# A hand-ordered attention and feed-forward kernel: a new order list, with two groups of seven block products fewer and another opening

## The chip, the cores and the metric

The kernel runs on one core of one Trainium2 chip. The metric is the device time of one execution in microseconds (us); lower is better. The core has a TensorE for matmuls (PE; its weight loads are shown apart as PEld and overlap with the matmuls), a VectorE (DVE), a ScalarE (ACT), a GpSimd (POOL) and a SyncE (SP) that issues DMAs. Each engine works through its own instructions strictly in order. 16 DMA engines move data; DMAs are issued in the queues of SP, POOL and ACT.

## The reference

Queries and keys are each assigned to the nearest of 16 centroids of their head. Attention is taken only between queries and keys of the same cluster. The result, with the heads side by side, goes through a feed-forward layer with a SiLU.

```python
batch, n_heads, seq, head_dim = (4, 8, 768, 64); n_clusters = 16
q_assign = np.argmax(np.einsum('bhsd,hcd->bhsc', q_n, c_n), axis=-1)   # q_n, c_n: unit length
k_assign = np.argmax(np.einsum('bhsd,hcd->bhsc', k_n, c_n), axis=-1)
mask = q_assign[:, :, :, None] == k_assign[:, :, None, :]
scores = np.where(mask, scale * np.matmul(q, k.transpose(0, 1, 3, 2)), -1000000000.0)
attn = np.exp(scores - np.max(scores, axis=-1, keepdims=True))
attn = attn / (np.sum(attn, axis=-1, keepdims=True) + 1e-09)
attn_out = np.matmul(attn, v)
x = attn_out.transpose(0, 2, 1, 3).reshape(3072, 512)
h = x @ w_in            # 512 x 2048
g = h * (1.0 / (1.0 + np.exp(-h)))
out = g @ w_out         # 2048 x 512
```

## The kernel before, in words

**Order by hand.** The tile scheduler is off (`manual_schedule`). A long list of words, `order` (lines 813 to 954), is read from front to back by the loop at the end of the function; each word is looked up in the table `words` and issues the instructions of one small step. An engine gets its instructions in the order of the words that have work for it, and semaphores see to it that data are there and buffers free. So the list fixes the order on every engine and in every DMA queue, and nothing else decides when a step runs: a word runs as soon as everything ahead of it on its own engine is done and its inputs and its buffer are there, wherever it stands among words of other engines. A letter at the end of some words names the engine: A for ACT, D for DVE, P for POOL, S for SP's queue. A number behind `@` is the PSUM bank (0 to 3) that a step of PE writes.

**Attention words.** There are 32 heads (4 batches of 8), numbered i; jobs 0 to 7 and `x0`, `x1` are the first batch in smaller pieces.
- `ld.i` (`load`, line 102) asks SP for the raw q and k of a job; jobs 0 to 7 are asked for ahead of the list, job 0 in ACT's queue. Raw buffers are shared: job 8 takes the one of job 2, job 9 that of job 3, job 10 of 4, job 11 of 5, job 12 of 6; `x0` and `x1` take those of jobs 0 and 1.
- `hi.i` (line 114) copies raw to 16 bits (ACT line 120, POOL line 122 or DVE line 124); `lo.i` (DVE, line 129) makes the rest that the 16 bits leave out. Four `hl` buffers go round.
- `tr.i` (PE, line 152) transposes both and `ev.i` (ACT line 161 or DVE line 163) brings the result from PSUM to SBUF; from job 8 on `tp.i` (line 138) does both by a DMA transpose in SP's queue.
- `L.i` (PE, line 176) multiplies with the centroids; `ls`, `mx`, `ge` (DVE) add the halves, find the largest and write the one-hot code of the cluster.
- The code goes beside q and k as extra rows, so that the scores of other clusters come out far below the rest: `cd` (PE), `ce` (ACT or DVE) and `cg` (DMA, SP, line 260), or for heads 0 and 3 `ct` (PE) with `cq` (ACT) and `ck` (DVE, line 278), without a DMA; later jobs use `sc` (POOL), `cx` (SP) and `mv` (DMA from SP or POOL).
- `s.u` (PE, line 353) makes the scores of unit u (two matmuls of 384 columns), `x.u` (ACT, line 358) their exp. 192 units; in the first batch units 0 to 2 are head 0, 3 to 5 head 1 and so on up to 23, and 24 to 47 are the second half of its queries.
- `v.i` loads v (SP or POOL queue; five buffers go round) and `vc.i` (POOL, line 294) casts it; `pv` (PE, line 370) sums exp times v, `nm` (DVE) divides, `xp`/`xe` or `xd` transpose the result into the feed-forward's input.

**Feed-forward words.** The first product has 16 blocks of 128 columns for each half batch (`b.c`).
- A plain unit computes one block for 384 rows: `au.b.c.f`, or `ab` and `ae` for its first three matmuls and its last (PE, line 418), then `t` (tanh on ACT, line 438) and `g` (gate on DVE, line 441).
- A group `b.c.s` computes four blocks (columns 2s, 2s+1 and both eight further) from seven products of 2 by 2 blocks instead of eight (class `Quad`): `q...1` to `q...7` (PE, line 547, four matmuls of 192 columns each), `qc` (copies, ACT line 557 or DVE 559), `qa` (sums, DVE line 564), `qt` and `qg` (tanh on ACT, line 571, gate on DVE, line 584), or `qz` (ACT, line 576) at the end. It needs sums of weight blocks (`un`, DVE) and differences of input blocks (`tt`, DVE, line 507).
- `b` and `be` (plain), or the `Pair` steps `ps`, `pp`, `p1`, `pa`, `pu`, `pc`, `pd` make the second product; `bs`, `pf`, `pe`, `pm`, `py` store.
- `w.0` to `w.7` load the eight pieces of w_in, `w.8` to `w.11` the four of w_out, by POOL's queue; `w.10.22` first waits for the exp of unit 22 on POOL, and `w.11.23` for that of unit 23.

`j.3` are three idle matmuls, `cn`, `c5`, `kd`, `sk` prepare the centroids, `od` clears a code buffer on POOL.

## Time and profile before

| what | value |
|---|---|
| median of 3 runs | 295.29 us (294.81 to 296.18) |
| the profiled execution | 294.78 us |
| its span | 292.9 us |
| instructions | 8949 |
| PE busy | 283.7 us, 97% |
| DVE busy | 260.1 us, 89% |
| ACT busy | 246.8 us, 84% |
| POOL busy | 62.9 us, 21% |
| moved by DMA | 45.21 MB, mean 154 GB/s |

The profile is of one execution. Its time is 1.9 us more than its span; that part lies around the span and is in no view. PE's busy time counts matmuls whose ends are modelled, so that a stretch shown as busy can hide short gaps. In the views below an engine name with a q (SPq, POOLq) is its queue of issues and waits; `out<-in` are the program's names of tiles; a number in brackets after `<-` is idle time of the engine just before an instruction, with what ended it.

### The profile page before, as it was taken

The numbers are of one execution on the slowest core, as the hardware profiler recorded it, in microseconds if no ns is written. First come the engines' busy times: TensorE is split into PE (matmuls) and PEld (weight loads), VectorE is DVE, ScalarE is ACT, GpSimd is POOL, SyncE is SP. The second block draws the span as 40 slices with busy tenths as digits, with TensorE's granted clock in tenths as the row PEclk, the third lists the DMA queues.
The fourth block names the chain that finished last, engine by engine and source line by source line (L and its number), as shares of the span: only waits on it lengthen the run. The fifth ranks groups of instructions, "written<-read, shape, count | busy, mean of one in ns | idle before, by whom it ended". The sixth has DMA issues, their size and how long they took to land.

```text
span 292.9 us, 8949 instructions
## 1 busy us (share of the span) xinstructions
PE 283.7 (97%) x3561; PEld 222.8 (76%) x3561; DVE 260.1 (89%) x579; ACT 246.8 (84%) x430; POOL 62.9 (21%) x118
## 2 busy tenths in 40 slices
...
GB/s 212 301 212 145 174 217 287 192 187 231 234 264 140 202 223 236 188 185 82 198 147 221 185 230 218 133 77 52 187 63 66 2 113 24 87 2 36 39 40 142
DMA packets 80394, 45.21 MB, mean 154 GB/s; under 512 B 58368, under 2 KB 76736, under 8 KB 80352
## 3 DMA queue, kind: packets, MB, share of 16 engines
...
## 4 chain that ended last, share of the span: by engine, by line
PE 72%; DMA 9%; DVE 7%; ACT 7%; SPq 2%; issue 2%; ACTq 0%; DVEq 0%
PE po L683 18%; PE pS L353 16%; PE pO L370 10%; PE qa L547 8%; DMA raw<-in_k_dram 8%; PE ph L418 6%; PE qg L547 4%; PE po L596 4%; ACT P L358 3%; PE psN L176 2%; PE qb L547 2%; DVE hl L129 2%; SPq L108 1%; DMA raw<-in_q_dram 1%; ACT hl L120 1%
## 5 line engine op out<-in xcount | busy, mean ns | idle before, releaser
L358 ACT ACTIVATE P<-pS 128x768 f16<-128x768 f32 x192 | 150.4, 821 | 14.5 <-PE pS L353 12.7
L353 PE MATMUL pS<-ab 128*128 128x384 f16 x384 | 88.4, 326 | 1.1 <-ACT P L358 0.9
L353 PEld LDWEIGHTS <-ab 128*128 128x128 f16 x384 | 34.1, 98 | 12.8 <-issue 1.9
L370 PEld LDWEIGHTS <-P 128*128 128x128 f16 x1152 | 40.1, 97 | 4.9 <-ACT P L358 0.2
L370 PE MATMUL pO<-vt,P 128*128 128x65 f16 x1152 | 41.6, 193 | 0.2
L294 POOL CAST vt<-vn 128x384 f16<-128x384 f32 x32 | 21.4, 681 | 73.8 <-PE pO L370 39.5
L683 PEld LDWEIGHTS <-gt 128*128 128x128 f16 x328 | 31.7, 98 | 4.9
L547 PEld LDWEIGHTS <-ws 128*128 128x128 f16 x352 | 30.3, 98 | 5.0 <-issue 0.8
L418 PE MATMUL ph<-xt,win_s 128*128 128x384 f16 x160 | 31.9, 326 | 0.4 <-DVE cc L564 0.4
L129 DVE SCALAR_TENSOR_TENSOR hl<-raw,hl 128x768 f16<-128x768 f32 (+3 forms) x35 | 31.4, 902 | 0.9 <-ACT hl L120 0.8
L584 DVE SCALAR_TENSOR_TENSOR gt<-tn,cc 128x384 f16<-128x384 f32 x48 | 26.4, 558 | 2.1 <-ACT tn L571 2.0
L683 PE MATMUL po<-wout_s,gt 128*128 128x256 f16 x216 | 27.5, 273 | 0.0
L571 ACT ACTIVATE tn<-cc 128x384 f32<-128x384 f32 x48 | 25.3, 534 | 2.3 <-DVE gt L584 1.1
L547 PEld LDWEIGHTS <-win_s 128*128 128x128 f16 x264 | 22.9, 98 | 4.1 <-issue 0.3
L596 PE MATMUL po<-wout_s,gt 128*128 128x512 f16 x96 | 24.5, 379 | 0.1
L418 PEld LDWEIGHTS <-win_s 128*128 128x128 f16 x160 | 15.4, 98 | 9.9 <-issue 0.6
L441 DVE SCALAR_TENSOR_TENSOR gt<-tn,ph 128x384 f16<-128x384 f32 x40 | 21.7, 548 | 0.7 <-ACT tn L438 0.3
L547 PE MATMUL qa<-tt,ws 128*128 128x192 f16 x176 | 21.4, 246 | 0.4 <-ACT cc L557 0.4
L438 ACT ACTIVATE tn<-ph 128x384 f32<-128x384 f32 x40 | 20.1, 509 | 0.9 <-PE ph L418 0.6
L176 PEld LDWEIGHTS <-ab 128*128 128x128 f16 x458 | 16.8, 97 | 4.0 <-DMA ab<-hl 0.4
L220 POOL TENSOR_SCALAR od<-od 128x96 f16<-128x96 f16 x16 | 8.7, 547 | 47.2 <-DVE od L213 47.1
L382 DVE TENSOR_TENSOR xn<-pO,zr 128x384 f16<-128x384 f32 x32 | 17.8, 558 | 1.1
...
## 6 DMA issues: line engine op xcount, KB each, us to landing
raw<-in_k_dram SPq DMA_DIRECT2D x31, 192.0 KB, 4.0
out_dram<-ot SPq DMA_DIRECT2D x23, 256.0 KB, 2.4
raw<-in_q_dram SPq DMA_DIRECT2D x24, 192.0 KB, 4.3
vn<-in_v_dram SPq DMA_DIRECT2D x21, 192.0 KB, 4.2
vn<-in_v_dram POOLq DMA_DIRECT2D x11, 192.0 KB, 4.5
win_s<-in_moe_w_in_dram POOLq DMA_DIRECT2D x8, 256.0 KB, 6.8
...
cp<-gt SPq DMA_DIRECT2D x4, 256.0 KB, 4.7
```

The source lines that it names most:

```text
L129: nc.vector.scalar_tensor_tensor(out=hl[:, s, 1, :], in0=raws[job.name][:, s, :], scalar=QS, in1=hl[:, s, 0, :], op0=ALU.mult, op1=ALU.sub ...
L176: nc.tensor.matmul(L[:, n % g, :, n // g], ab[:, i, :], stk[:, job.groups[i // 3][0], x : x + w], start=(x == 0), stop=(x + w == 2 * HC),)
L353: nc.tensor.matmul(pS[:, e, 0:HALF], abs_[kj.name][:, kn, :], rhs, start=True, stop=True)
L358: nc.scalar.activation(out=P, in_=pst.pop(u)[:, :, 0:HALF], func=AF.Exp, bias=0.0, scale=ESC)
L370: nc.tensor.matmul(o[:, (2 * t + h) * VW : (2 * t + h + 1) * VW], Ps[i + h, c, j // 2][:, j % 2, ts(t, 128)], vtb[(i + h) % 13][:, j, 0:VW ...
L418: nc.tensor.matmul(ph[:, 0:HALF], win_s[:, r, ts(fb, 128)], xts[b, c][:, r, :], start=(r == 0), stop=(r == NR - 1))
L441: nc.vector.scalar_tensor_tensor(out=gt[:, fb, :], in0=tn, scalar=1.0, in1=ph[:, 0:HALF], op0=ALU.add, op1=ALU.mult)
L547: nc.tensor.matmul(o[:, g * QT : (g + 1) * QT], w, y, start=(k in (1, 2, 5) and g == 0 and r == 0), stop=(r == 1), skip_group_check=True,)
L571: nc.scalar.activation(out=t, in_=self.src(n), func=AF.Tanh, bias=0.0, scale=1.0)
L584: eng.scalar_tensor_tensor(out=self.gt[:, f : f + 2, h], in0=self.tn[n].rearrange("p (g n) -> p g n", g=2), scalar=1.0, in1=self.src(n).re ...
L596: nc.tensor.matmul(po, gts[b, c][:, fc, ts(t, 128)], wout_s[:, fc, :], start=(fc == 0), stop=(fc == NFB - 1))
L683: nc.tensor.matmul(o, l[:, f, :], x, start=(f == 0 and k in begins), stop=(f == HK - 1), skip_group_check=True)
```

## The change

Only the list `order` changes (lines 813 to 954, 1796 words, become 813 to 952, 1774 words). No function is touched.

- The groups 0.0.0 and 0.0.1 go (22 groups become 20): 14 `q` words, six `qc`, six `qa`, eight `qt`, eight `qg`, and the four `tt.0.0`. In their place stand eight plain units, `au.0.0.0` to `3` and `8` to `11`, with their `t` and `g`. The `un` words stay, since later groups use the same sums.
- The opening is in another order. `s.0` stands ahead of `L.2` and `tr.5`. `hi.5` and `hi.6` go from ACT to POOL. `v.1` and `v.10` come first among the loads of v, `v.10` from POOL. `w.1` is POOL's second DMA, `w.4` and `w.6` follow behind `hi.6` and `v.3`, then `w.0`, `w.5`, `w.3`, `w.2`, `w.7`; `w.9` and `w.8` stand behind `vc.7`, `w.10` and `w.11` later still. `ld.8`, `ld.9`, `ld.11` move up between `cg.1` and `v.2` in SP's queue.
- Steps change engine. `hi`: 18 on ACT, 14 on DVE, 3 on POOL become 12, 18, 5. `ce`: 10 on ACT and 6 on DVE become 8 and 8. `qc`: 37 and 29 become 33 and 27. `xe`: 5 and 5 become 4 and 6. One `be` goes to DVE. `v`: 21 by SP and 11 by POOL become 14 and 18. `mv`: 7 by SP and 9 by POOL become 2 and 14.
- The rest of the list holds the same steps in another order, with other banks. At the end the pair `3.1.x` is stored (`pe.3.1.x`) just ahead of the last product of the pair `3.1.p`; before, that store stood earlier.

The beginning and the end of the list:

```diff
@@ -811,146 +811,144 @@
 
     order = """
-        hi.0.A.K lo.0.K hi.0.A.Q lo.0.Q tr.0.q@1 hi.1.A j.3@2 cn tr.0.k@3 hi.2.A ev.0.k.A c5@02 lo.1 kd sk ev.0.q.A
-        v.4.S lo.2 hi.4.A hi.3.P v.0.S tr.1.kq@32 ld.x0 L.0.16@0 ev.1.k.D ev.1.q.A v.1.S tr.2.kq@13 mx.0 v.5.S ge.0
-        L.1.16@2 ev.2.k.A lo.4 v.2.S ct.0@01 ev.2.q.A mx.1 cq.0 ge.1 L.2.16@3 ck.0 hi.5.A cd.1 tr.4.kq@01 vc.4 ce.1.A
-        lo.5 ev.4.q.A cg.1 vc.0 lo.3 hi.7.A tr.5.kq@21 ld.x1 mx.2 s.0 ev.5.k.A ev.5.q.D s.1 ge.2 tr.3.kq@12 ev.4.k.D
-        vc.1 x.0 cd.2 lo.7 v.3.P L.4.16@0 ce.2.A ev.3.q.A ev.3.k.D cg.2 tr.7.kq@32 hi.6.A hi.x0.P mx.4 L.3.16@1 v.6.S
-        ge.4 ev.7.q.A lo.6 v.7.S cd.4 x.1 s.2 L.5.16@2 ce.4.D x.2 ev.7.k.D od.0 cg.4 s.3 tr.6.kq@03 mx.3 x.3 hi.x1.P
-        ld.8 ge.3 s.4 ev.6.k.D x.4 ev.6.q.D s.5 mx.5 L.6.16@1 ge.5 x.5 s.6 mx.6 cd.5 w.3 ct.3@03 x.6 ge.6 lo.x0 cd.6
-        vc.2 s.7 cq.3 s.8 w.0 x.7 ce.5.D tr.x0.k@0 ck.3 vc.5 cg.5 L.7.32@2 ce.6.A vc.3 ls.7 pv.0.0.0.x@3 x.8 cg.6 s.9
-        vc.6 mx.7 tr.x0.q@1 x.9 w.1 ge.7 s.10 ev.x0.q.D cd.7 vc.7 pv.0.0.1.x x.10 ev.x0.k.D s.11 w.2 lo.x1 pv.0.0.2.x
-        ce.7.A w.5 L.x0.32.0.6@1 x.11 L.x0.32.6.12 cg.7 s.12 w.9 ls.x0 w.7 pv.2.0.0.x@0 x.12 s.13 mx.x0 w.6 pv.2.0.1.x
-        x.13 ge.x0 w.4 pv.2.0.2.x nm.0.0 cd.x0 s.14 w.8 ce.x0.A tr.x1.k@2 x.14 s.15 cg.x0 ev.x1.k.D x.15 s.16
-        tr.x1.q@3 x.16 L.x1.32.0.6@1 s.17 ev.x1.q.D x.17 L.x1.32.6.12 s.18 ls.x1 pv.4.0.0.x@2 x.18 nm.2.0 s.19
-        pv.4.0.1.x x.19 mx.x1 s.20 xp.2.0@3 pv.4.0.2.x ge.x1 x.20 xe.2.0.D xp.0.0@0 s.21 nm.4.0 s.22 x.21 pv.6.0.y.0@3
-        xe.0.0.D x.22 xp.4.0@2 s.23 xe.4.0.D ab.0.0.7@0 hi.8.D x.23 w.10.22 cd.x1 s.24 pv.6.0.y.1 x.24 w.11.23 s.25
-        nm.6.0 ab.0.0.6@2 x.25 s.26 ce.x1.D xp.6.0@3 x.26 cg.x1 s.27 xe.6.0.D ld.11 q.0.0.0.1@1 ae.0.0.6 x.27 tt.0.0.3
-        ld.10 qc.0.0.0.1.A v.10.S s.30 ae.0.0.7 tt.0.0.1 tt.0.0.2 tt.0.0.4 q.0.0.0.2@3 t.0.0.6 qa.0.0.0.1 g.0.0.6
-        t.0.0.7 g.0.0.7 un.1.0 un.1.1 s.28 x.28 ab.0.0.5@3 ae.0.0.5 t.0.0.5 g.0.0.5 q.0.0.1.1@0 x.30 ab.0.0.4@2
-        ae.0.0.4 q.0.0.0.5@3 qt.0.0.0.0 un.2.0 q.0.0.0.6 ld.9 v.17.S un.2.1 t.0.0.4 s.29 un.4.0 qc.0.0.0.5.A un.3.0
-        s.34 q.0.0.0.3 qc.0.0.0.2.A g.0.0.4 q.0.0.0.7 qg.0.0.0.0 qa.0.0.0.3 q.0.0.1.2@2 qc.0.0.1.1.A qa.0.0.1.1 un.3.1
-        q.0.0.1.6 x.29 ld.12 s.32 qt.0.0.0.1 qt.0.0.1.0 q.0.0.1.5@3 qg.0.0.0.1 au.0.0.12@2 qc.0.0.1.5.A qc.0.0.1.2.A
-        q.0.0.1.7 qg.0.0.1.0 x.32 qa.0.0.0.2 un.4.1 t.0.0.12 q.0.0.0.4 v.13.S q.0.0.1.3 qa.0.0.1.2 s.37 qa.0.0.1.3
-        qt.0.0.0.3 qg.0.0.0.3 g.0.0.12 q.0.0.1.4 qt.0.0.1.3 au.0.0.13@3 lo.8 hi.9.D tp.8 hi.10.D hi.11.A t.0.0.13
-        pv.0.1@1 qg.0.0.1.3 b.0.0.0.0@2 lo.11 g.0.0.13 tp.11 b.0.0.0.1 x.37 x.34 nm.0.1 lo.10 qt.0.0.1.1 qt.0.0.0.2
-        qg.0.0.0.2 s.33 s.31 x.33 b.0.0.0.2 x.31 lo.9 s.41 x.41 au.0.0.14@0 s.35 qg.0.0.1.1 t.0.0.14 g.0.0.14 hi.12.D
...
-        pf.3.1.x ps.3.1.p.4 pp.3.1.x.3 pd.3.1.x pe.3.1.x pa.3.1.p pu.3.1.p pp.3.1.p.7 pc.3.1.p pp.3.1.p.3 pf.3.1.p
-        pp.3.1.p.4 pl.3.1.p pz.3.1.p py.3.1.p pm.3.1.p
+        hi.0.A.K lo.0.K hi.0.A.Q lo.0.Q tr.0.q@1 v.1.S v.10.P cn hi.1.A tr.0.k@3 v.4.S ev.0.k.A lo.1 v.0.S hi.2.A lo.2
+        j.3@2 c5@03 kd tr.1.kq@32 ev.1.k.D sk w.1 ev.0.q.A ev.1.q.A L.0.16@1 mx.0 tr.2.kq@03 hi.4.A ge.0 ev.2.k.A lo.4
+        hi.3.P hi.5.P ld.x0 L.1.16@2 mx.1 ct.0@10 ev.2.q.A ge.1 ck.0 cq.0 tr.4.kq@31 ev.4.k.D cd.1 ce.1.A ld.x1 lo.5
+        s.0 L.2.16@0 mx.2 ev.4.q.A cg.1 ge.2 x.0 L.4.16@3 hi.7.A lo.3 tr.5.kq@21 cd.2 ld.8 ce.2.A cg.2 ev.5.q.D s.1
+        ev.5.k.A s.2 hi.6.P w.4 mx.4 lo.7 ge.4 tr.3.kq@10 ev.3.k.A ev.3.q.A tr.7.kq@21 lo.6 x.1 vc.1 ev.7.q.D ev.7.k.D
+        cd.4 ce.4.A ld.9 L.3.16@0 mx.3 ge.3 L.5.16@1 mx.5 x.2 cg.4 ld.11 tr.6.kq@23 ev.6.k.D v.3.P ev.6.q.D s.3 s.5
+        v.2.S w.6 L.6.16@2 x.3 vc.0 ge.5 mx.6 cd.5 ge.6 x.5 ce.5.D s.4 cg.5 v.5.S vc.4 hi.x0.P hi.x1.P L.7.32@3 cd.6
+        ce.6.D x.4 s.6 x.6 pv.0.0.0.x@1 w.0 s.8 x.8 ct.3@20 vc.10 lo.x0 w.5 w.3 s.7 pv.0.0.1.x pv.0.0.2.x od.0 cq.3
+        x.7 s.12 vc.3 ls.7 x.12 tr.x0.k@2 ck.3 s.10 mx.7 cg.6 v.6.S x.10 lo.x1 tr.x1.q@0 s.11 x.11 ge.7 cd.7 vc.2
+        ev.x0.k.D nm.0.0 tr.x0.q@2 s.9 x.9 ev.x0.q.D tr.x1.k@1 ce.7.D cg.7 s.14 x.14 L.x0.32.0.6@2 L.x0.32.6.12 s.16
+        x.16 pv.2.0.0.x@3 hi.8.D ls.x0 s.13 x.13 pv.2.0.1.x mx.x0 ge.x0 v.11.P s.15 x.15 pv.2.0.2.x s.17 x.17 cd.x0
+        ev.x1.k.D s.18 w.2 ev.x1.q.D x.18 hi.9.D ce.x0.D vc.5 pv.4.0.0.x@0 s.19 x.19 w.7 pv.4.0.1.x s.20 x.20
+        pv.4.0.2.x lo.8 nm.2.0 v.7.S s.21 x.21 xp.2.0@1 nm.4.0 xe.2.0.D cg.x0 tp.8 xp.0.0@3 xe.0.0.D s.23 x.23 ld.10
+        L.x1.32.0.6@2 L.x1.32.6.12 ls.x1 vc.6 s.22 x.22 pv.6.0.y.0@0 s.29 x.29 xp.4.0@1 xe.4.0.A vc.7 un.3.0
+        pv.6.0.y.1 s.34 mx.x1 ge.x1 ld.12 un.1.1 nm.6.0 cd.x1 ce.x1.D s.27 x.34 cg.x1 x.27 ab.0.0.7@3 xp.6.0@0
+        xe.6.0.D s.26 x.26 un.1.0 au.0.0.0@2 t.0.0.0 lo.9 tp.9 g.0.0.0 ae.0.0.7 ab.0.0.4@1 t.0.0.7 ae.0.0.4 t.0.0.4
+        g.0.0.4 s.24 x.24 s.28 un.2.0 x.28 hi.10.D hi.11.D w.9 g.0.0.7 ab.0.0.5@2 hi.12.D au.0.0.2@0 t.0.0.2 g.0.0.2
+        s.25 ae.0.0.5 x.25 t.0.0.5 g.0.0.5 w.8 s.35 au.0.0.15@1 x.35 s.30 lo.10 pv.0.1@3 t.0.0.15 nm.0.1 x.30 s.31
+        x.31 ab.0.0.6@0 ae.0.0.6 g.0.0.15 t.0.0.6 g.0.0.6 s.36 x.36 tp.10 lo.12 au.0.0.10@2 ld.14 t.0.0.10 au.0.0.9@1
+        t.0.0.9 g.0.0.9 g.0.0.10 au.0.0.1@3 t.0.0.1 g.0.0.1 s.42 s.46 x.42 L.8.32@0 ls.8 x.46 lo.11 au.0.0.13@1 ld.13
+        t.0.0.13 v.8.P g.0.0.13 au.0.0.14@2 t.0.0.14 s.32 x.32 au.0.0.11@3 t.0.0.11 mx.8 ge.8 s.39 x.39 tp.11
+        au.0.0.12@1 t.0.0.12 s.33 g.0.0.11 g.0.0.14 w.10.22 w.11.23 x.33 vc.11 tw.0.0.6 au.0.0.3@0 s.41 t.0.0.3
+        g.0.0.3 tp.12 x.41 au.0.0.8@3 g.0.0.12 t.0.0.8 g.0.0.8 vc.8 s.38 L.9.32@2 hi.13.A pv.2.1@0 x.38 s.43 x.43
+        cd.8@1 tw.0.6.2 od.1 b.0.0.0.0@3 un.4.0 nm.2.1 v.13.S ls.9 mx.9 s.37 x.37 ce.8.D b.0.0.0.1 vc.13 hi.14.D s.40
+        ge.9 lo.13 L.11.32@0 lo.14 s.47 ld.15 xp.0.1@1 ld.17 xe.0.1.D x.47 b.0.0.1.0@2 b.0.0.1.1 b.0.0.1.2 ls.11 mx.11
...
+        pp.3.1.p.1@5 pp.3.1.x.2@0 pp.3.1.p.5@6 ps.3.1.p.3 pa.3.1.x pc.3.1.x pf.3.1.x p5.3.1.p p1.3.1.p pp.3.1.p.6
+        pp.3.1.p.3 pu.3.1.p pl.3.1.p pm.3.1.p pa.3.1.p ps.3.1.x.4 pp.3.1.p.7 pc.3.1.p pf.3.1.p pp.3.1.x.4 pp.3.1.x.3
+        pd.3.1.x pe.3.1.x pp.3.1.p.4 pz.3.1.p py.3.1.p
     """.split()
```

224 lines of the change are left out of this document (110 added, 114 removed).

## The prediction

> **What bounds the kernel now.** I read the page first, then busy time by stage, the chain of waits, the timeline of the first 60 us, the DMA view of the early stretch and the groups by line. From the page:
>
> ```profile
> span 292.9 us, 8949 instructions
> ...
> PE 283.7 (97%) x3561; PEld 222.8 (76%) x3561; DVE 260.1 (89%) x579; ACT 246.8 (84%) x430; POOL 62.9 (21%) x118
> ```
>
> TensorE (PE) is busy for 97% of the span, but that is an average over stages. The busy time by stage (stretch, its length, then busy time and count of PE, PEld, DVE, ACT and POOL, the granted clock, the share of the DMA engines, GB/s) shows where the other 3% lie:
>
> ```profile
> 0.00:14.10 14.10, 10.79 (x133) 6.91 (x134) 10.03 (x41) 10.25 (x19) 5.08 (x15) 1.00 0.83 256
> 14.10:39.00 24.90, 24.24 (x406) 18.63 (x405) 20.73 (x50) 23.86 (x37) 17.87 (x25) 1.00 0.94 182
> 39.00:58.60 19.60, 18.04 (x185) 12.08 (x183) 17.93 (x40) 17.83 (x35) 0.00 (x0) 1.00 1.12 234
> 58.60:289.50 230.90, 230.60 (x2847) 185.18 (x2843) 211.38 (x452) 194.46 (x343) 39.98 (x78) 1.00 0.65 139
> 16.00:22.00 6.00, 5.93 (x104) 4.57 (x102) 5.84 (x15) 5.89 (x10) 5.97 (x5) 1.00 0.72 205
> ```
>
> From 58.6 to 289.5 us PE idles for 0.30 us of 230.90. There a new order can win next to nothing, however much it takes off ScalarE (ACT) and VectorE (DVE), and it can lose. What can be won lies earlier: 3.31 us up to the first exp at 14.1, 0.66 from there to 39, and 1.56 from 39 to 58.6. The stretch from 14.1 to 39 is as much ACT's as PE's: 23.86 of 24.90 us.
>
> What holds PE up after 39 us is in the chain of waits (start, us, what) and, below it, in the timeline (start, us, engine and operation, in brackets the idle time before it and what ended that):
>
> ```profile
> 39.48 6.45 DMA raw<-in_k_dram
> ...
> 45.95 6.77 DMA raw<-in_k_dram
> ```
> ```profile
> 52.48 1.03 DVE L124 TENSOR_SCALAR hl<-raw 128x768 f16<-128x768 f32 x2 [1.44 <-DMA raw<-in_k_dram]
> ...
> 55.28 0.48 PE L353 MATMUL pS<-ab 128*128 128x384 f16 x2 [0.65 <-ACT P L358]
> ```
>
> The chain does not run through PE here but through loads of k that are asked for at 39.48 and 45.95 us. DVE waits 1.44 us for one of them, ACT's exp comes late behind DVE, and PE waits 0.65 us for ACT. Those loads share the DMA engines with the weights. The DMA view from 21 to 55 us (q0 is POOL's queue, q1 is SP's; packets, MB and share of the engines' time, then issues with KB each and the median us to landing):
>
> ```profile
> q0 software_dynamic: 3264, 4.20, 76.1%
> q1 hardware_dynamic: 2702, 2.62, 30.5%
> ...
> win_s<-in_moe_w_in_dram POOLq DMA_DIRECT2D x8, 256.0 KB, 6.8
> ...
> raw<-in_k_dram SPq DMA_DIRECT2D x4, 192.0 KB, 8.4
> ...
> ab<-cd SPq DMA_DIRECT2D x2, 48.0 KB, 6.2
> ```
>
> and over the whole run, where most loads have no weights beside them:
>
> ```profile
> raw<-in_k_dram SPq DMA_DIRECT2D x31, 192.0 KB, 4.0
> ...
> out_dram<-ot SPq DMA_DIRECT2D x23, 256.0 KB, 2.4
> ...
> ab<-cd SPq DMA_DIRECT2D x10, 48.0 KB, 4.1
> ...
> out_dram<-ot ACTq DMA_DIRECT2D x1, 128.0 KB, 1.7
> ```
>
> **The change part by part.** *Products.* Two groups, 28 matmuls of 192 columns each, become eight plain units of four matmuls of 384 columns. The chain shows both kinds back to back:
>
> ```profile
> 80.80 0.66 PE qa L547 x8
> ...
> 83.29 1.30 PE ph L418 x8
> ```
>
> Removed are 56 x 0.66/8 = 4.62 us, added 32 x 1.30/8 = 5.20 us: **+0.6 us** of work on PE, which bounds the kernel.
>
> *ACT, DVE and POOL.* In the groups by line (count, then busy time and the mean ns of one, then idle time before them):
>
> ```profile
> L571 ACT ACTIVATE tn<-cc 128x384 f32<-128x384 f32 x48 | 25.3, 534 | 2.3 <-DVE gt L584 1.1 <-DVE cc L564 0.9
> ...
> L438 ACT ACTIVATE tn<-ph 128x384 f32<-128x384 f32 x40 | 20.1, 509 | 0.9 <-PE ph L418 0.6
> ...
> L120 ACT ACTIVATE hl<-raw 128x768 f16<-128x768 f32 (+3 forms) x18 | 13.7, 760 | 2.1 <-DMA raw<-in_q_dram 1.3 <-DMA raw<-in_k_dram 0.7
> ...
> L557 ACT ACTIVATE cc<-qa 128x384 f32<-128x384 f32 x26 | 12.5, 492 | 1.0 <-PE qa L547 0.9
> ...
> L564 DVE TENSOR_TENSOR cc<-qb,cc 128x384 f32<-128x384 f32 x22 | 12.1, 552 | 1.2 <-PE qb L547 0.8
> ...
> L124 DVE TENSOR_SCALAR hl<-raw 128x768 f16<-128x768 f32 x14 | 7.8, 562 | 1.4 <-DMA raw<-in_k_dram 1.4
> L122 POOL TENSOR_SCALAR hl<-raw 128x768 f16<-128x768 f32 (+1 forms) x3 | 7.0, 2337 | 3.1 <-DVE hl L129 3.1
> ```
>
> ACT loses six `hi` copies net (6 x 0.760 = 4.6 us) and four group copies net (4 x 0.492 = 2.0; six go, two come over from DVE); its eight tanh of groups become eight of units, 8 x 0.025 = 0.2 less. With a few small copies more it has some 7 us less to do. DVE loses the groups' six sums and those two copies (8 x 0.552 = 4.4) and takes four `hi` (4 x 0.562 = 2.2): some 2 us less. POOL takes two `hi` at 2.3 us each, seven more loads of v and five more moves of codes. Behind 58.6 us all this is worth 0, because PE covers it; it would cost up to 1 us if POOL's queue came late with a v or a code there. In the opening it counts where ACT is what is waited for.
>
> *First scores.* The timeline of the opening:
>
> ```profile
> 3.71 0.57 POOL L781 TENSOR_TENSOR cy<-cs,hf 128x1 f32<-128x1 f32 x1 [1.80 <-DVE cs L779]
> ...
> 7.38 2.16 POOL L122 TENSOR_SCALAR hl<-raw 128x576 f16<-128x576 f32 x1 [3.10 <-DVE hl L129]
> ...
> 8.37 0.69 ACT L120 ACTIVATE hl<-raw 128x576 f16<-128x576 f32 x1
> ...
> 10.92 0.62 DVE L278 TENSOR_SCALAR ab<-pC 16x256 f16<-16x256 f16 x2
> 11.05 0.69 ACT L120 ACTIVATE hl<-raw 128x576 f16<-128x576 f32 x1
> ...
> 12.85 0.51 PEld L152 LDWEIGHTS <-hl 128*128 128x128 f16 x9 [1.03 <-DVE hl L129]
> ...
> 13.37 0.81 PE L353 MATMUL pS<-ab 128*128 128x384 f16 x4
> ...
> 14.11 0.80 ACT L358 ACTIVATE P<-pS 128x768 f16<-128x768 f32 x1
> ...
> 15.76 0.77 POOL L289 DMA_DIRECT2D vn<-in_v_dram  x1
> ...
> 18.48 1.04 PE L353 MATMUL pS<-ab 128*128 128x384 f16 x4
> ```
>
> The first score needs the code that DVE writes in `ck.0`, done at 10.92 + 0.62 = 11.54. In the old list it stands behind `tr.5`, which waits 1.03 us for `lo.5` and starts at 12.85, so it comes at 13.37. The new list puts `s.0`, `L.2` and `L.4` between `cd.1` and `tr.5`, and on ACT it takes `hi.5`, `hi.7` and `ev.5.k` from ahead of the first exp. The first score can then start near 11.7 and the first exp near 12.5, and the hole in PE is filled: **-1.0 us** (0 to -1.3). `hi.5` is made on POOL now, after `hi.3`, and is ready at 7.38 + 2 x 2.16 = 11.70; ACT had it ready at 11.05 + 0.69 = 11.74. That move costs nothing as long as its data are there.
>
> *Early transfers.* `v.10` and `w.1` come first in POOL's queue, right behind `cy`, so they go out at about 4.3 and 4.9 us. In the old list POOL's first transfer was issued at 15.76. From the DMA rows above q0 moves 4.20/(0.761 x 34 us) = 0.162 MB in a microsecond of all engines, so `w.1` (256 KB) is worth 1.6 us of them; `v.10` (192 KB) at q1's 2.62/(0.305 x 34) = 0.25 MB is worth 0.8. Up to 2.4 us of transfers are set among the loads of jobs 2 to 7. The price is 0 if ACT and DVE come later than the data anyway. It is at most about 1.8, if what is left of those loads moves at half speed while POOL's run. `hi.4` starts at 8.37 without a wait now, so there is no long wait to hide it behind but some time in hand, and I take **+0.8**, near the middle. [...]
>
> *39 to 58.6 us.* `ld.8`, `ld.9` and `ld.11` move up, to where jobs 2, 3 and 5 give their buffers back, and into a stretch in which the DMA engines have room (0.72 busy from 16 to 22 us). Six of the eight w_in pieces stand ahead of POOL's `od.0` instead of none, and `w.8` and `w.9` behind them. The groups' chains of copy, sum, tanh and gate are gone from this stage. So the waits before 52.48 and 55.28 should go. Late next is DVE, with 17.93 us of work in 19.60. I take PE's visible idle time there as won: **-1.6 us** (0 to -2.6; busy time is modelled, and gaps that it hides can go too).
>
> *The end.* A 256 KB store of the other pair is now issued at about the time of the last one, and by the rows above it takes 2.4 us where that takes 1.7: **+0.3 us** (0 to 0.7).
>
> The sum is 0.6 - 1.0 + 0.8 - 1.6 + 0.3 = -0.9 us. The profiled execution took 294.78 us (its span and 1.9 around it), 0.5 below the median of 295.29. Set against the median, the forecast is **294.4 us**.
>
> **The rivals.** *A, the early transfers hide.* ACT and DVE come late enough in the opening that no load is missed, and the stage from 39 us loses its hidden gaps too: 0.6 - 1.0 + 0 - 2.6 + 0.2 = -2.8, so 292.5. For it speaks the room on the DMA engines from 16 to 22 us. Against it speak the 2.1 us that ACT's `hi` copies already wait, for loads of q and k.
>
> *B, slower, by the shared DMA engines.* `w.1` and `v.10` push the loads of jobs 3 to 7 back by 1.8 us, and nothing of the first hole is won. With them comes `cg.1`, head 1's code, which stands behind five larger loads in SP's queue, and which takes 6.2 us beside weights against 4.1. It decides from the point where that code lands after PE reaches `s.3` (18.48 now): then PE and ACT stand still, for up to 6.2 - 4.1 = 2.1 us, of which I count 1.5. 0.6 + 0 + 1.8 + 1.5 - 1.6 + 0.3 = +2.6, so 297.9. For it also speaks that `cg.6` waits behind `v.5` in SP's queue, whose buffer is free only after `vc.10`, behind two `hi` on POOL.
>
> *C, the gain only moves.* ACT is as full as PE from 14 to 39 us, so scores made sooner wait for it there, and half of the later waits come back with other names: 0.6 + 0 + 0.8 - 0.8 + 0.3 = +0.9, so 296.2.
>
> **How the numbers follow.** The forecast has a chance of 0.36, A 0.27, B 0.22, C 0.15. A measurement of this kernel tells about 0.5% (1.5 us) from no change, so faster is under 293.8 and slower over 296.8. The forecast's own range, its terms half-way to their bounds, is 293.2 to 295.7, and a quarter of it is faster. Faster: 0.27 + 0.09 = 0.36. Slower: 0.20 of the 0.22 of B and a quarter of C, 0.24. The rest, 0.40, is the same. The range reaches past A's and B's values, to 291.6 and 298.0.
>
> **What would show it.** Right: the first score near 11.7 and the first exp before 13 us, no DVE wait for raw between 45 and 58 us, PE idle for under 0.5 us from 39 to 58.6, and 0.6 us more work of PE. Wrong: ACT idle before `hi.4` for raw, `s.3` held up by a code that has not landed, the first exp later than 13.5 us, or more than 1 us of idle PE after 60 us.

## The result, and the profile after

The kernel after takes 299.25 us (median of 6 runs, 297.38 to 301.24), the kernel before, on the same chip, 295.40 (6 runs, 294.81 to 296.18). The ratio is 1.0124, with a 95% interval from 1.0078 to 1.0169: slower by 3.9 us, and outside the forecast's range. The medians here and below are over all runs, while the ratios leave out single runs more than 1.5% above the fastest of their kernel. The profiled execution of the kernel after is its longest, 301.24 us, so about 2 us of what its trace shows are not in the median.

From its page, the span and the busy times:

```profile
span 299.4 us, 8877 instructions
...
PE 285.2 (95%) x3537; PEld 223.2 (75%) x3537; DVE 260.5 (87%) x575; ACT 238.8 (80%) x416; POOL 73.0 (24%) x132
```

ACT has 8.0 us less to do (some 7 were forecast), and PE 24 matmuls fewer (56 removed, 32 added). Neither sets the time. The busy time by stage, in the columns and stretches shown of before:

```profile
0.00:14.10 14.10, 10.11 (x102) 6.26 (x103) 8.34 (x37) 8.04 (x15) 5.62 (x16) 0.98 0.80 225
14.10:39.00 24.90, 21.65 (x352) 17.00 (x351) 21.66 (x47) 19.84 (x30) 17.99 (x22) 0.87 1.00 230
39.00:58.60 19.60, 19.60 (x209) 13.26 (x207) 18.15 (x39) 19.09 (x34) 5.57 (x11) 1.00 1.20 194
...
58.60:289.50 230.90, 227.43 (x2822) 181.18 (x2820) 208.37 (x446) 191.08 (x337) 43.84 (x84) 1.00 0.63 136
```

In the stage that the change was to win, from 39 to 58.6 us, PE was busy for 18.04 us and is now for all 19.60. The opening to 39 us, which was to win 1 us, loses 0.7 and 2.6 us of busy time, and behind 58.6 us, where nothing was to be lost, 3.47 us are idle (0.30 before).

The first loss begins with the loads of job 4. From the timeline of the opening:

```profile
10.94 0.69 ACT L120 ACTIVATE hl<-raw 128x576 f16<-128x576 f32 x1 [1.94 <-DMA raw<-in_q_dram]
...
12.37 0.50 PE L267 MATMUL pC<-ident,om 128*16 128x128 f16 x6 [2.03 <-ACT ab L161]
...
13.22 3.27 POOL L122 TENSOR_SCALAR hl<-raw 128x576 f16<-128x576 f32 x2 [4.23 <-DMA raw<-in_q_dram]
...
13.54 0.81 PE L353 MATMUL pS<-ab 128*128 128x384 f16 x2
...
14.48 0.80 ACT L358 ACTIVATE P<-pS 128x768 f16<-128x768 f32 x1
```

`hi.4` waits 1.94 us on ACT for raw q, `ev.2.k`, next on ACT, starts only at 11.53, and PE waits 2.03 us for the bank that it empties. `hi.5` on POOL waits 4.23 us for its data. The first score comes at 13.54, no sooner than before (13.37). The DMA view from 3 to 15 us shows the loads late (issues, KB each, median us to landing), after:

```profile
raw<-in_k_dram SPq DMA_DIRECT2D x5, 192.0 KB, 7.3
```

and before:

```profile
raw<-in_k_dram SPq DMA_DIRECT2D x5, 192.0 KB, 3.7
```

The second loss, from the timeline of 45 to 66 us (SPq is SP's DMA queue):

```profile
45.23 12.69 SPq L138 DMA_TRANSPOSE ab<-hl  x2
...
60.24 0.44 SPq L108 DMA_DIRECT2D raw<-in_k_dram  x1
...
61.09 0.52 PE L176 MATMUL psN<-stk,ab 128*128 128x32 f16 x12 [1.18 <-DMA ab<-hl]
...
64.54 0.84 ACT L120 ACTIVATE hl<-raw 128x768 f16<-128x768 f32 x1 [3.99 <-DMA raw<-in_k_dram]
...
66.14 0.48 PE L353 MATMUL pS<-ab 128*128 128x384 f16 x2 [2.13 <-ACT P L358]
```

The transposes of jobs 9 and 10 hold SP's queue for 12.69 us (4.65 and 7.26 of issue). The loads of job 13 stand behind them, ACT waits 3.99 us in `hi.13` with its exps behind it, and PE waits twice, for the transpose and for an exp. The four pieces of w_out go out at 39.69 to 42.79, into that stretch; in the kernel before they went out at 27.49 to 36.95, and the three transposes began at 51.07 and held the queue for 8.60 us:

```profile
51.07 8.60 SPq L138 DMA_TRANSPOSE ab<-hl  x3
```

### The profile page after: what moved, and what is told of

It reads as the page before. It is cut to its first block, busy times and chain, and to the rows that moved or that the text cites. A ratio compares the mean times of both kernels' runs of the same rounds, so it can differ in the third digit from the quotient of the medians.

```text
span 299.4 us, 8877 instructions
## 1 busy us (share of the span) xinstructions
PE 285.2 (95%) x3537; PEld 223.2 (75%) x3537; DVE 260.5 (87%) x575; ACT 238.8 (80%) x416; POOL 73.0 (24%) x132
## 4 chain that ended last, share of the span: by engine, by line
PE 80%; DMA 9%; DVE 4%; ACT 3%; issue 1%; SPq 1%; POOL 1%; ACTq 0%; POOLq 0%
PE po L683 18%; PE pS L353 18%; PE pO L370 10%; PE qa L547 9%; PE ph L418 8%; PE po L596 7%; PE qg L547 4%; DMA raw<-in_q_dram 4%; DMA ab<-cd 3%; PE psN L176 3%; PE qb L547 2%; DVE hl L129 2%; DMA raw<-in_k_dram 1%; ACT P L358 1%; DVE gt L441 1%
## 5 line engine op out<-in xcount | busy, mean ns | idle before, releaser
L353 PE MATMUL pS<-ab 128*128 128x384 f16 x384 | 89.8, 329 | 3.9 <-ACT P L358 2.1
L418 PE MATMUL ph<-xt,win_s 128*128 128x384 f16 x192 | 37.9, 326 | 0.0
L129 DVE SCALAR_TENSOR_TENSOR hl<-raw,hl 128x768 f16<-128x768 f32 (+3 forms) x35 | 33.1, 948 | 3.6 <-ACT hl L120 2.6
L547 PEld LDWEIGHTS <-ws 128*128 128x128 f16 x320 | 27.4, 98 | 3.4 <-issue 0.2
L441 DVE SCALAR_TENSOR_TENSOR gt<-tn,ph 128x384 f16<-128x384 f32 x48 | 25.7, 549 | 1.3 <-ACT tn L438 1.0
L584 DVE SCALAR_TENSOR_TENSOR gt<-tn,cc 128x384 f16<-128x384 f32 x42 | 23.8, 571 | 2.2 <-ACT tn L571 2.0
L438 ACT ACTIVATE tn<-ph 128x384 f32<-128x384 f32 x48 | 24.3, 515 | 1.1 <-PE ph L418 1.0
L571 ACT ACTIVATE tn<-cc 128x384 f32<-128x384 f32 x42 | 22.0, 533 | 0.3 <-DVE cc L564 0.2
L547 PE MATMUL qa<-tt,ws 128*128 128x192 f16 x160 | 19.2, 246 | 0.0
L176 PE MATMUL psN<-stk,ab 128*128 128x32 f16 (+1 forms) x458 | 18.1, 189 | 1.2 <-DMA ab<-hl 1.2
```

Of the source, the lines that this page charges most:

```text
L129: nc.vector.scalar_tensor_tensor(out=hl[:, s, 1, :], in0=raws[job.name][:, s, :], scalar=QS, in1=hl[:, s, 0, :], op0=ALU.mult, op1=ALU.sub ...
L176: nc.tensor.matmul(L[:, n % g, :, n // g], ab[:, i, :], stk[:, job.groups[i // 3][0], x : x + w], start=(x == 0), stop=(x + w == 2 * HC),)
L353: nc.tensor.matmul(pS[:, e, 0:HALF], abs_[kj.name][:, kn, :], rhs, start=True, stop=True)
L418: nc.tensor.matmul(ph[:, 0:HALF], win_s[:, r, ts(fb, 128)], xts[b, c][:, r, :], start=(r == 0), stop=(r == NR - 1))
L438: nc.scalar.activation(out=tn, in_=ph[:, 0:HALF], func=AF.Tanh, bias=0.0, scale=1.0)
L441: nc.vector.scalar_tensor_tensor(out=gt[:, fb, :], in0=tn, scalar=1.0, in1=ph[:, 0:HALF], op0=ALU.add, op1=ALU.mult)
```

## The experiments

The theory to begin with was the first loss above: the early transfers push the raw loads back. Its rivals were the second loss (w_out and the transposes), the copies moved to POOL, and, as the runs went on, the volume of the transfers as a whole (theory D).

All kernels change the order list alone, unless said otherwise. Medians with the ratio to the kernel before on the same chip and its interval:

| kernel | us | ratio (95%) |
|---|---|---|
| after | 299.25 | 1.0124 (1.0078 to 1.0169) |
| `w.1` later | 298.96 | 1.0106 (1.0062 to 1.0151) |
| `v.10` later | 299.30 | 1.0125 (1.0089 to 1.0161) |
| both later | 298.64 | 1.0103 (1.0061 to 1.0146) |
| w_out sooner | 307.32 | 1.0404 (1.0371 to 1.0438) |
| job 13's loads sooner | 299.70 | 1.0147 (1.0098 to 1.0196) |
| both later, codes first | 299.46 | 1.0125 (1.0067 to 1.0183) |
| w_out behind exp 36 | 307.35 | 1.0396 (1.0347 to 1.0446) |
| both later, codes first, job 13's loads sooner | 299.55 | 1.0136 (1.0078 to 1.0195) |
| after, no weights loaded | 291.83 | 0.9889 (0.9858 to 0.9921) |
| before, no weights loaded | 294.18 | 0.9973 (0.9949 to 0.9998) |
| before with units | 302.09 | 1.0243 (1.0207 to 1.0278) |
| before, loads early | 294.39 | 0.9971 (0.9948 to 0.9993) |
| after, no w_in | 300.83 | 1.0144 (1.0089 to 1.0200) |
| after, no w_out | 298.40 | 1.0119 (1.0075 to 1.0164) |
| transposes late, w_out sooner | 305.11 | 1.0323 (1.0281 to 1.0365) |
| before, loads and score early | 294.57 | 0.9995 (0.9969 to 1.0021) |
| after, less asked for early | 296.69 | 1.0062 (1.0037 to 1.0087) |
| before with extra loads | 299.48 | 1.0124 (1.0083 to 1.0165) |

**The early transfers moved back.** Theory 1 was rival B's mechanism: `v.10` and `w.1` delay the raw loads.

```diff
-hi.0.A.K ... v.1.S v.10.P cn ... sk w.1 ev.0.q.A ... hi.6.P w.4 ... v.3.P ev.6.q.D
+hi.0.A.K ... v.1.S cn ... sk ev.0.q.A ... hi.6.P w.1 w.4 ... v.3.P v.10.P ev.6.q.D
```

> The kernel after, with one piece of w_in (`w.1`, 256 KB) asked for next to `w.4` and not ahead of `hi.3` on POOL. Theory 1 (the two early transfers push the loads of jobs 4 to 7 back): those loads land about 1.6 us sooner, the q part of job 4 by 9.5 us in place of 10.86, PE's hole at 10.3 to 12.4 us shrinks to about 1 us, and the time falls by 1 to 2 us, to 297.3 to 298.3. Theory 2 (what is lost is lost near 60 us, to the late w_out) and theory 3 (the loss is the move of `hi.5` and `hi.6` to POOL): the time stays within 0.5 us of 299.25.

> The kernel after, with `v.10` asked for behind `v.3` on POOL and not ahead of `hi.3`; `v.5` then takes the buffer of head 4's v and no longer that of head 10's. Theory 1: the loads of jobs 4 to 7 land about 0.8 us sooner, and the time falls by 0.5 to 1.5 us; with v.5, cg.6, v.7 no longer held by vc.10, the codes of heads 6 and 7 and the w_out pieces come sooner too, which by theory 2 gives another 1 us or more. By theory 3 the time stays within 0.5 us of 299.25.

> Both moves at once. Theory 1: no transfer of POOL's among the loads of jobs 4 to 7, which land as in the kernel before (7.7 to 11 us); no hole of PE at 10.3 to 12.4, first score near 12, granted clock 1.0 throughout; the time falls by 2.5 to 4 us, to 295.3 to 296.8. Theory 2: the opening gives under 1 us and 3 us of PE's waits near 60 us stay. Theory 3: 299.25 within 0.5.

Neither move alone, nor both, gave what theory 1 said: the medians are 0.3, 0 and 0.6 us lower, and all three ratios lie in the interval of the change. With both moved, the opening is as it should be. From the timeline of that kernel, the first score, then a later one:

```profile
11.86 0.50 PE L353 MATMUL pS<-ab 128*128 128x384 f16 x2
...
22.79 0.50 PE L353 MATMUL pS<-ab 128*128 128x384 f16 x2 [2.19 <-DMA ab<-cd]
```

The hole of 2 us is gone from 10.3 us and has come back at 20.6. There PE waits for head 2's code, asked for at 15.54 and landed at 22.75. So the place was right and the gain was not: the DMA engines still had as much to move. The copies `hi.5` and `hi.6` are still POOL's here, so they did not make the hole of the opening.

**w_out sooner.**

```diff
-w.7 ... vc.6 ... vc.7 ... hi.11.D w.9 g.0.0.7 ... g.0.0.5 w.8 s.35
+w.7 w.9 w.8 ... vc.6 ... vc.7 ... hi.11.D g.0.0.7 ... g.0.0.5 s.35
```

> The kernel after, with `w.9` and `w.8` (pieces of w_out) asked for right behind `w.7` on POOL, ahead of the casts of the v of heads 6 and 7 that wait for their data, so that they go out near 31 us and not near 40. Theory 2: the DMA transposes tp.9 and tp.10 (issues of 4.65 and 7.26 us now) take under 3 us each, the loads of jobs 13 and 14 go out before 55 us and not at 58 to 60, PE's 3.3 us of waits between 58.6 and 66 us go, and the time falls by 2 to 3.5 us, to 295.8 to 297.3. Theory 1 alone: the opening's 4 us stay and the time falls by at most 0.5 us.

The opposite of theory 2: 8 us slower than the kernel after. The pieces went out from 32.22 and met the transpose of job 8, issued at 35.44, which landed at 52.11 (at 41.19 in the kernel after); that of job 9 took 10 us of issue. PE then waited 6.36 us at once, and behind that wait the granted clock was 0.50 from 54 to 62 us, so that a part of the 8 us is matmuls at half the clock. Going out sooner meant meeting the transposes sooner.

**Single waits taken away.** In the kernel after, `ld.13` ahead of the transposes; in the kernel with both early transfers later, the codes ahead of `ld.8`, `ld.9`, `ld.11`; and all of these together.

```diff
-cg.x1 ... lo.9 tp.9 ... tp.10 ... ld.14 ... lo.11 au.0.0.13@1 ld.13
+cg.x1 ... lo.9 ld.13 tp.9 ... tp.10 ... ld.14 ... lo.11 au.0.0.13@1
```
```diff
-cg.1 ... ld.8 ce.2.A cg.2 ... ce.4.A ld.9 ... cg.4 ld.11 ... cg.5 v.5.S ... cg.6 v.6.S
+cg.1 ... ce.2.A cg.2 ... ce.4.A ... cg.4 ld.8 ... cg.5 ld.9 v.5.S ... cg.6 ld.11 v.6.S
```

> The kernel after, with the two loads of job 13 (`ld.13`) asked for ahead of the DMA transposes of jobs 9 and 10 in SP's queue and not behind them; their buffer is free since `lo.7`. Theory S (SP's queue stands in the two transposes, 4.65 and 7.26 us of issue, and ACT stands in `hi.13` behind the loads that come after them, with its exps behind it): ACT's 3.99 us of idle time before `hi.13` go, PE's 3.3 us of waits between 58.6 and 66 us fall to about 1.2 (the wait of `L.9` for its transpose), and the time falls by 2 us, to 297.2. Theory D (the DMA engines are full up to 60 us, and what one transfer wins another loses): it falls by under 0.7 us.

> The kernel with both early transfers moved back (298.64 us), and `ld.8`, `ld.9`, `ld.11` asked for behind the codes of heads 4, 5 and 6 and not ahead of those of heads 2, 4 and 5. Theory C (a code of 48 KB takes as long as the larger loads that stand ahead of it in SP's queue): the code of head 2, 7.2 us from issue to landing there, takes about 4, PE's 2.35 us wait for it at 20.4 us goes, and the time falls by 1.5 to 3 us, to 295.6 to 297.1. Theory D: another wait takes its place, and it falls by under 0.7 us.

> `w.1` and `v.10` later, the codes ahead of `ld.8`, `ld.9`, `ld.11`, and `ld.13` ahead of the transposes. If theories C and S hold, the gains add: 298.6 - 2 - 1.5 = about 295, as fast as the kernel before. By theory D it stays above 297.5.

All three stay between 299.4 and 299.7: theories S and C fall as explanations of the time, though each wait went where it was taken away. ACT's wait in `hi.13` is gone with `ld.13` early, and PE waits 1.74 us up to 64.86 for a transpose that landed at 64.81 instead. With the codes first, head 2's code takes 6.2 us in place of 7.2, and two other codes hold PE up for 2.22 us up to 32.7 and 2.24 us up to 37.3. The second of them needs 9.68 us from issue to landing.

**w_out held back.**

```diff
-hi.11.D w.9 ... g.0.0.5 w.8 s.35 ... x.36 tp.10 ... g.0.0.14 w.10.22 w.11.23 ... vc.11 tw.0.0.6
+hi.11.D ... g.0.0.5 s.35 ... x.36 w.9.36 w.8.36 w.10.36 w.11.36 tp.10 ... g.0.0.14 ... vc.11
```

> The kernel after, with the four pieces of w_out held back until the exp of unit 36 (at 51.6 us there) and not issued at 39.7 to 42.8; the copies of w_out for the later products stand behind the next exps. Theory T (the w_out pieces of POOL's queue slow the DMA transposes of jobs 9 and 10 and so SP's queue): those two take under 3 us of issue each, the loads of jobs 13 and 14 go out before 53 us, ACT does not wait for job 13, and PE's waits between 58.6 and 66 us are those for w_out alone, which lands near 62; the time falls by 1 to 3 us. If the transposes stay above 4 us each, something else slows them.

(`tw.0.0.6`, a copy of w_out, moves behind `cd.8`.) Theory T holds for the transposes and not for the time, 307.35. Before the first piece goes out at 51.80, the transposes take 2.13, 1.45 and 1.44 us of issue; behind it the next two take 4.94 and 7.13. The pieces land at 58.7 to 70.1, where PE needs them from 60. Here too the clock is 0.50 behind the waits, from 70 to 76 us.

**No weights at all.** Each piece is set to a constant by POOL where it was asked for, in both kernels.

```diff
-            nc.gpsimd.dma_start(win_s[:, r, fs], moe_w_in[128 * r : 128 * r + 128, fs])
+            nc.gpsimd.memset(win_s[:, r, fs], 0.01)
```

> The kernel after with no transfer of w_in or w_out: each piece is set to a constant by POOL where it was asked for, so 4 MB less go through the DMA engines before 62 us; all else is as in the kernel after. Theory D (up to 60 us the transfers share the engines, and what is asked for early makes the codes, loads and transposes late that are due first): PE's holes at 10.3, 28, 36.9 and 59 to 66 us nearly all go, and the kernel after is no slower than the kernel before under the same edit: 290 to 292.5. Theory Q (the order of the instructions on SP, POOL, ACT and DVE is worse in itself): at least 2 us of holes stay, and it is 2 us or more slower than the kernel before under the same edit.

> The same edit in the kernel before, for comparison: it loses the waits of its stage from 39 to 58.6 us (1.6 us visible, up to 2.6) and perhaps 0.5 in the opening: 291.5 to 293.5. By theory D it is within 1 us of the kernel after without weights or slower than that one; by theory Q it is faster than that one by 2 us or more.

This turns the order round: 291.83 against 294.18. The two intervals do not touch. Without weights the change wins 2.4 us, with them it loses 3.9. So theory Q falls: the order on the engines is not worse in itself, nor are the products. The kernel before gains less than was expected of it (294.18, where 291.5 to 293.5 was written): from 39 to 58.6 us PE still idles for 1.67 us in it. The DMA engines' share (last column but one) fits theory D; after without weights, then before without weights:

```profile
0.00:14.10 14.10, 11.28 (x150) 7.48 (x151) 9.95 (x40) 9.48 (x18) 9.08 (x18) 1.00 0.82 252
14.10:39.00 24.90, 24.40 (x392) 18.28 (x390) 23.71 (x57) 23.78 (x36) 23.83 (x27) 1.00 0.65 181
39.00:58.60 19.60, 19.18 (x195) 12.29 (x194) 18.72 (x38) 18.49 (x33) 4.75 (x8) 1.00 0.63 136
```
```profile
0.00:14.10 14.10, 10.85 (x133) 6.82 (x134) 9.95 (x40) 10.42 (x20) 6.04 (x15) 1.00 0.80 258
14.10:39.00 24.90, 23.60 (x395) 17.73 (x394) 21.96 (x47) 22.88 (x35) 22.30 (x22) 1.00 0.26 76
39.00:58.60 19.60, 17.93 (x170) 12.26 (x171) 19.12 (x43) 18.18 (x35) 3.91 (x4) 1.00 0.57 154
```

Share times length, summed to 58.6 us: 11.6 + 16.2 + 12.3 = 40.1 us of the engines without weights after, 11.3 + 6.5 + 11.2 = 29.0 before. With weights the kernel before has 11.7 + 23.4 + 22.0 = 57.1, so the weights take about 28. Before, 29 + 28 fit into 58.6 us; after, 40 + 28 do not. (Shares reach 1.20 above, so the sum is rough.) The new list asks for some 11 us worth of loads, v and transposes sooner than it was, above all between 14 and 39 us, where the weights went.

**Which weights.** The same edit for w_in alone and for w_out alone.

> The kernel after with the eight pieces of w_in set to a constant and not loaded; w_out is loaded as in the kernel after. If w_in is what costs (opening and codes, 10 to 38 us): the holes there go and those at 59 to 66 us stay, 294 to 296. If w_out beside the transposes is what costs: at least 297.5.

> The kernel after with the four pieces of w_out set to a constant and not loaded; w_in is loaded as in the kernel after. If w_out beside the transposes is what costs: the transposes of jobs 9 and 10 take under 3 us of issue each (4.65 and 7.26 in the kernel after), the waits at 59 to 66 us go, 294.5 to 296. If w_in is what costs: at least 297.5.

The two do not part the cause. Without w_out the kernel is as slow as the change; without w_in it is no faster either, but there w_out goes out sooner, so that it does not show what w_in alone costs. Without w_out the waits behind 58.6 us go (PE is busy for 7.40 of 7.40 us up to 66) and those of the opening stay. Without w_in, the pieces of w_out go out from 31.96 and meet the transposes of jobs 8 and 9, as in "w_out sooner" (its six runs spread from 296.5 to 302.4; the profile is of a long one, 302.15). The landing times of the transposes, DMA view from 35 (for no w_in: 30) to 62 us, for the kernel after, without w_out and without w_in:

```profile
ab<-hl SPq DMA_TRANSPOSE x4, 8.4
```
```profile
ab<-hl SPq DMA_TRANSPOSE x5, 3.8
```
```profile
ab<-hl SPq DMA_TRANSPOSE x4, 7.6
```

**Kept apart.** Both early transfers later, w_out whole behind `w.7`, and job 8's transpose behind the loads of jobs 10, 12 and 13.

```diff
-w.7 ... cg.x0 tp.8 ... ld.10 ... ld.12 ... cg.x1 ... lo.9 tp.9
+w.7 w.9 w.8 w.10 w.11 ... cg.x0 ... ld.10 ... ld.12 ... cg.x1 ... lo.9 ld.13 tp.8 tp.9
```

> All transfers kept, but w_out and the transposes apart: `w.1` and `v.10` later, the four pieces of w_out together right behind `w.7` on POOL (from about 30 us), job 8's DMA transpose behind the loads of jobs 10, 12 and 13 (near 44 us and not 35). If their meeting is what costs, transposes take under 3 us of issue and the time falls from 298.6 (both early transfers moved back) to 294 to 296.5. If the volume of the transfers before 60 us costs wherever it lies, waits for codes and loads from 32 to 45 us take the place of those saved: 298 or more.

305.11: the late transpose of job 8 still took 4.92 us beside the last pieces, from 50.7 us PE stood for 5.28 us behind a gate of DVE, and the clock was 0.50 from 54 to 60 us. With everything kept, no placing of w_out that I tried was better than that of the change.

**The products alone, and two parts in the kernel before.**

```diff
-q.0.0.0.1@1 ... tt.0.0.3 ... qc.0.0.0.1.A ... q.0.0.0.2@3 ... qa.0.0.0.1 ... qg.0.0.1.2
+au.0.0.0@1 t.0.0.0 g.0.0.0 ... au.0.0.8@3 t.0.0.8 g.0.0.8 ...
```

> The kernel before with the products of the change alone: its first two groups of four (seven products each) become eight plain units, set where the products of the groups stood, and the rest of the list stays. By the prediction's sum of products it does 0.6 us more work on PE; with fewer copies and sums around them it comes to 295.0 to 296.2. If it is over 297, the loss of the change is in its products; if it is under 294.5, the units were a gain that the new order spoils.

302.09, 7 us slower. By what was written ahead of the run this would put the loss into the products. The trace speaks against it, because the place is bad: the units come one behind the other and wait for a bank. From its timeline:

```profile
49.28 0.81 PE L418 MATMUL ph<-xt,win_s 128*128 128x384 f16 x4 [2.32 <-DVE gt L441]
```

And with the weights left out the new list, with the same units spread out, is the faster one. What the units are worth in the old order stays open.

```diff
-cg.1 ... ce.2.A ... cg.2 ... cg.4 ... ld.8 ... cg.5 ... ld.11 ... ld.9
+cg.1 ... ce.2.A ... ld.8 cg.2 ... ld.9 cg.4 ... ld.11 cg.5
```
```diff
-tr.5.kq@21 ld.x1 mx.2 s.0 ev.5.k.A ... vc.1 x.0
+s.0 x.0 tr.5.kq@21 ld.x1 mx.2 ev.5.k.A ... vc.1
```

> The kernel before with the loads of jobs 8, 9 and 11 asked for where the change asks for them, ahead of the codes of heads 2, 4 and 5 in SP's queue (not after head 4's, and at 39 to 46 us), and nothing else changed. Theory C (a code waits for the larger loads ahead of it): the codes of heads 2 to 6 land 1 to 4 us later, PE waits for at least one of them between 18 and 37 us, what it wins from 39 to 58 us (up to 1.6) it loses there: 295 to 297.5. Without theory C: the waits from 39 to 58 us go and nothing takes their place, 293.5 to 294.3.

> The kernel before with the loads of jobs 8, 9 and 11 early (294.39 us), and with the first score ahead of `tr.5` on PE and its exp right behind it in the list. By the prediction's step (1 us of PE's hole at 11.8 us filled) it comes to 293.4 to 293.9. If ACT, which is as full as PE from 14 to 39 us, only waits elsewhere, it stays at 294.2 to 294.6.

The early loads cost nothing here (294.39), although some 3 us of transfers (four loads of 192 KB at 0.77 us each, an estimate from the 0.25 MB in a microsecond that the prediction reads off its DMA view) come from behind 39 us into the stretch before it. PE waits for a code once, 0.45 us. The ratio, 0.9971, is the lowest of the kernels with all their work, but the kernel that adds the first score does not repeat it (294.57, 0.9995). There the first score comes at 11.91 in place of 13.37, and adds nothing. Nor do the loads win the stage from 39 us by themselves. DVE's wait of 1.44 us for raw is gone, and PE is busy for 18.23 us where it was for 18.04:

```profile
39.00:58.60 19.60, 18.23 (x185) 12.55 (x184) 18.87 (x41) 18.58 (x34) 0.00 (x0) 1.00 1.01 203
```

PE waits there for a sum (0.39 us), a gate (0.46) and a copy (0.41).

**More and less asked for early.** The last two test the volume. In the kernel after, the v of heads 10 and 11 (two loads of 192 KB) go from before 40 us to behind 64 us, `w.1` from 5 to 13 us, and `ld.8`, `ld.9`, `ld.11` stand behind the codes of heads 4, 5 and 6. In the kernel before, 1.5 MB more are loaded.

```diff
-v.10.P ... w.1 ... hi.6.P w.4 ... vc.10 ... v.11.P ... vc.11 ... vc.13
+... hi.6.P w.1 w.4 ... vc.13 v.11.P vc.11 v.10.P vc.10
```
```diff
+        nc.sync.dma_start(spare[0][:, n, :], nat(k, 20 + n, 0, 6))
...
-cg.2 ... cg.4 ... cg.5 ... cg.6
+cg.2 dd.0 dd.1 ... cg.4 dd.2 dd.3 ... cg.5 dd.4 dd.5 ... cg.6 dd.6 dd.7
```

> The kernel after, with `w.1` next to `w.4`, the v of heads 10 and 11 asked for (and cast) only behind head 13's, near 66 us, and `ld.8`, `ld.9`, `ld.11` behind the codes of heads 4, 5 and 6. Without weights the engines move 40.1 us worth of transfers before 58.6 us in the kernel after and 29.0 in the kernel before (DMA shares of the stages times their lengths), and the weights take some 28 more: 68 and 57 us worth in 58.6. If the volume decides, 2 us less of it before 40 us gives 1 to 2.5 us: 296 to 298. If only the opening's order decides, about 298.6, as with both early transfers moved back.

> The kernel before with eight more loads of 192 KB in SP's queue, two behind each code of heads 2, 4, 5 and 6, into a buffer that nobody reads: 8 x 0.77 = 6.1 us worth of transfers more between 18 and 40 us, and no other instruction moved. If the volume decides, codes and loads come up to 6 us later and the time rises by 2 to 6 us, to 297 to 301. If there is room for it, it stays within 0.6 us of 294.9.

Both came out as the volume theory said. The kernel before with the extra loads takes 299.48, the ratio of the change itself (1.0124). No engine instruction was moved; codes land later and PE waits. From its DMA view from 14 to 39 us and its timeline:

```profile
ab<-cd SPq DMA_DIRECT2D x5, 40.0 KB, 6.5
...
ab<-cd SPq DMA_DIRECT2D x1, 48.0 KB, 10.0
```
```profile
34.17 0.82 PE L360 MATMUL pS<-ab 128*128 128x384 f16 x2 [2.96 <-DMA ab<-cd]
```

(Line 360 there is line 353 of the others.) In the same stretch a code of 40 KB took 4.1 us in the kernel before, 4.6 after, and 3.0 after without weights. The extra loads also stand ahead of the next codes in SP's queue. The loads of jobs 8, 9 and 11 did so too, at no cost, but extra loads in another queue were not run, so that the volume and the place in the queue are not fully apart.

In the other direction, the kernel after with less asked for early takes 296.69 (295.27 before, on the same chip): by the ratios half of the loss is back, by the medians 2.4 us of the 3.9. It differs from "both later, codes first" (299.46) only in the v of heads 10 and 11; the two medians are 2.8 us apart for these two loads, though their intervals overlap. The traces show where: the same two scores wait for their codes in both, from "both later, codes first" and then from this kernel:

```profile
37.27 0.50 PE L353 MATMUL pS<-ab 128*128 128x384 f16 x2 [2.24 <-DMA ab<-cd]
```
```profile
35.13 0.50 PE L353 MATMUL pS<-ab 128*128 128x384 f16 x2 [1.51 <-DMA ab<-cd]
```

The score before each waits 2.22 and 0.60 us. From 30 to 39 us PE is busy for 4.54 and 6.88 us of 9.

## Why the prediction was wrong

The step that failed is the price of the *early transfers* (+0.8, at most 1.8), and with it the statement that behind 58.6 us the change is worth nothing, or at most 1 us. In their place the traces show PE's busy time down by 3.3 us up to 39 us and by 3.2 us from 58.6 to 66, because what the new list asks for early, as a whole, does not fit beside the weights.

*Early transfers* (+0.8, bounds 0 to 1.8). `w.1` and `v.10` were costed as two transfers on their own, in time of the engines. The loads behind them came later by more than their own length: the q part of job 4 at 10.86 (7.95 before), of job 5 at 13.05 (8.82), of job 7 at 14.66 (10.96), so 2.9 to 4.2 us. Beside POOL's queue a k load took 7.3 us instead of 3.7 (median of five, from 3 to 15 us). That the loads move at half speed beside POOL's transfers, on which the bound of 1.8 us and rival B's term rest, was an estimate: no run shows how the engines share their time between the queues, only that the loads landed these 2.9 to 4.2 us later. But the larger error was to stop there. Moving these two back won no more than 0.6 us, for the next transfer was late in their place. What had to be added up was everything that the new list asks for before PE needs the weights, 40 us worth beside 28, against the time. The prediction had the shares of 0.94 and 1.12 for the kernel before in its rows, took only a price per transfer from the DMA views, and called 16 to 22 us (0.72) room. That room is 1.7 us.

*39 to 58.6 us* (-1.6). The event was right: no DVE wait for raw is left, and PE is busy throughout. The reason was right in part at most. In the kernel before with the loads early the wait for raw is gone too, and PE's idle time there falls only from 1.56 to 1.37 us; without any weights it is 1.67. What is left are waits for copies, sums and gates, which the change takes out of this stage with the groups. PE also comes to this stage some 3 us late, which gives the other engines time, so how much of the 1.6 us is a gain is not shown.

*Behind 58.6 us*. Six pieces of w_in ahead of `od.0` and w_out behind them was written down as a gain. Nobody asked what w_out would meet: in the kernel before it was all but landed (53.77) when the transposes began (51.07), now it goes out between them. That cost 3.3 us up to 66, by a transpose, a queue behind it and a copy on ACT that stands ahead of exps. The prediction allowed 1 us, for POOL.

*First scores* (-1.0). The event was right once the early transfers are moved back: the first score comes at 11.86 and its exp at 12.62, where 11.7 and 12.5 were forecast. The worth was not: in the kernel before the same move gave nothing. Rival C's reason, that ACT is as full as PE there, fits; no run shows it by itself.

*Products and end.* With the weights left out PE is busy for 283.1 us in the kernel after and 283.2 in the kernel before, at a mean clock of 0.998 and 1.000: the 0.6 us more work do not show. At the end both kernels run 3.8 us past the start of their last matmuls (289.07 to 292.9, and 295.56 to 299.4): 0 in place of +0.3.

*Rivals.* B came nearest: slower, by shared DMA engines, with the loads pushed back and nothing of the first hole won. It had too few transfers in it (1.8 us) and kept the -1.6 of the later stage, which was given back behind it. Its other term, 1.5 us for head 1's code, is not what happened: that code took 5.3 us before and 5.7 after, and no wait of PE for a code stands in the trace before 38.70 us (1.57 us). With the weights left out in both kernels the change wins 2.4 us, near A's 2.8, but that is another comparison than A's.

Shown: that the loss comes with the weight transfers, that extra loads alone make one of the same size, that asking for less early brings about half of it or more back, and that w_out slows the transposes. Left open: how much of the loss with extra loads is their place in SP's queue and how much the halved clock (last section), the last 1.4 us of the kernel with less asked for early, and whether another list with these products would keep the gain; 296.69 is the best of them.
